# Two-layer decode kernel: row products queued behind the next unit's values, and a last projection in two rows of 256 columns

## The chip, the cores and the metric

The kernel runs on one core of a Trainium2 chip. The metric is the device time of one execution in microseconds. A core has a matrix engine (PE, with its weight loads shown apart as PEld), a vector engine (DVE), an activation engine (ACT), a general engine (POOL) and a sync engine (SP) that issues the transfers. Each engine works through its own instructions in order and waits on semaphores for the others. Matrix products land in PSUM, eight banks of 512 float32 columns on 128 partitions; everything else lies in SBUF.

## What is computed

A decode step for a batch of four tokens: attention with a cached K and V, then a gated feed-forward, and the same pair once more with the same weights and caches.

```python
def _A_ref(x, k_cache, v_cache, wq, wo):       # x (4,1,512), caches (4,8,8192,128)
    q = (x @ wq).reshape(B, Sq, 32, 128).transpose(0, 2, 1, 3)
    k = jnp.repeat(k_cache, 4, axis=1); v = jnp.repeat(v_cache, 4, axis=1)
    p = _softmax(jnp.einsum("bhqd,bhkd->bhqk", q, k) * (128 ** -0.5), axis=-1)
    o = jnp.einsum("bhqk,bhkd->bhqd", p, v)
    return o.transpose(0, 2, 1, 3).reshape(B, Sq, 32 * 128) @ wo     # wo (4096, 512)
def _B_ref(x, w_gate, w_up, w_down):           # 512 -> 1792 -> 512
    return (_silu(x @ w_gate) * (x @ w_up)) @ w_down
x = x + _A_ref(_layernorm(x), ...)
x = x + _B_ref(_layernorm(x), ...)
x = x + _A_ref(_layernorm(x), ...)
x = x + _B_ref(_layernorm(x), ...)
```

All inputs are bfloat16. The caches are 64 MB each in bfloat16 and are read in both layers, save a few pieces that stay on the chip between them.

## The kernel before

**Units.** The attention of a layer is cut into 16 units. Unit u = 4 gp + b holds two key-value heads (pair gp) of batch row b, with their 8 query heads. Its keys are one transfer of 4 MB and its values another. Layer 0 takes the units from 0 to 15, layer 1 in the order 15, 14, 13, 12, 0 to 11. The last transfers are cut into pieces: the values of the last unit come as 2048, 1536 and 512 KB. SP issues the transfers in a fixed list (`cmds`), each as soon as its slot in SBUF is free (`pump`, `freed`); the feed-forward weights of a layer follow the last values.

**A unit's steps.** DVE turns the keys in 8 pieces (`turn`, L488), PE makes the scores of each piece (`scores`, L512), DVE takes the maximum (L518, with a PE transpose L523 and L526), PE and ACT make the exponentials (`exps`, L549 to L561), DVE turns them (`turn_p`, L576), PE multiplies with the values in four parts (`products`, L643). DVE gathers the result (L687, L691), PE combines it (L696) and DVE scales it into `oT` (L701).

**The order of the work** is written out by a small planner. `blocks` holds the pieces of PE's main work, each counted at 0.9 us; the two newest are kept back (`LAG`). `line` is a queue of small steps, each with a gap; after every block the head's gap is lowered by 0.9, and it is issued when the gap is used up (`advance`). A part 3 of values puts the unit's gather and combine at the head of the line. `flush` issues steps at once, up to a tag or all of them.

**Output projection.** When the four units of a pair are done, `close_group` queues its projection with `wo`. The last pair of a layer is done directly (`project`, L767). Earlier ones are done as row products: `mix` (L721, L725) rearranges `oT`, `rows` (L747) makes eight products of 512 columns per pair, all summed in one row of bank OUTB, 4 by 512. After the last of these pairs `by_chunks` turns the row back to the layout of x: four times an ACT copy of 128 columns (L755) and a PE transpose (L757), in one step, and then DVE adds it to x (L711). Pairs 0 and 1 are queued together when pair 1 is done, with unit 7. In layer 0 pair 2 follows, and unit 13's keys, a piece of which is held in PSUM between the layers, issue all of `line` at their seventh block (`finished`, `hold`). In layer 1 pair 3 comes first, and pairs 0 and 1 are the last to go this way.

**The end.** After the last unit: `project`, the layer norm (`center`, L790 to L805, and `deviation`), gate and up products (L859), the gate function on DVE and ACT (L866 to L873), and the last projection. In layer 1 this gives x in rows straight away: `x_rows` (L785) first puts x into four quarter rows of bank STEP, each 4 by 128 on partitions 0, 32, 64 and 96, with float32 products by the identity; x_rows(0) is called between the products of the layer norm and the gate products, x_rows(1) between the up products and the last projection. Then 14 times four products (L880) add w_down; each quarter row takes 128 columns. DVE copies quarters 0 and 2 (L942), ACT 1 and 3 (L940), and SP writes the 4 by 512 result out.

Of the kernel before, what the change touches and what calls it, by code (L numbers as in the profile page):

```python
# [5 lines left out]
ACTF = mybir.ActivationFunctionType  # L6
# [97 lines left out]
def bass_interleave_layers__gqa_block_cached__swiglu_ffn__decode_kernel(  # L104
# [18 lines left out]
    P = 128  # L123
# [21 lines left out]
    with ExitStack() as es:  # L145
# [23 lines left out]
        def pick2(k):  # L169
            o = k // 2 * 2 * P + k % 2  # L170
            return slice(o, o + 2 * P - 1, 2)
# [74 lines left out]
        def bank(k):  # L246
            return ps[:, k * BANKF:(k + 1) * BANKF]
# [14 lines left out]
            assert o + b <= BANKF  # L262
            return bank(k)[rows, o + a:o + b], f"pb{k}"

        def quarter(j):
            return bank(STEP)[j * QB:j * QB + B, 0:P]

        sem = lambda name: es.enter_context(nc.semaphore(name))
        engines = {"pe": nc.tensor, "act": nc.scalar, "dve": nc.vector, "pool": nc.gpsimd, "sp": nc.sync}
# [356 lines left out]
        def values(L, u):  # L626
# [22 lines left out]
            def part(i):  # L649
                if i == 0:  # L650
                    flush(order[L][-1] if u == order[L][-2] else u)
                h = i // 2
                ts = range(i % 2 * (TB // 2), (i % 2 + 1) * (TB // 2))
                if not last or not h:
                    products(h, 0, QH, ts)
                elif i == 2:
                    gather(range(QH), ok, True)
                    fill(3)
                    products(h, 0, QH - 1, range(TB))
                    flush()  # L660
                    gather(range(QH - 1), ok2)
                else:
                    fill(1)
                    products(h, QH - 1, QH, range(TB))
                    fill(1)
                if i % 2:
                    finished(V(L, u), h * QH, (h + 1) * QH)
                if i == 3:
                    if p_name == "late":
                        freed(W_SLOT[L], NB, NB + 1)  # L670
                    done.add((L, u))
                    if last:
                        gather([QH - 1], ok3)
                        combine()
                    else:
                        line[0:0] = [[0.0, None, lambda: gather(range(QH), ok, True)], [1.3, None, combine]]
                    line.extend(behind.pop(u, []))
                    if all((L, gp * B + k) in done for k in range(B)):
                        close_group(L, gp, fill)

            into, iname = (acc2, "row") if last else (acc, "pb")

# [29 lines left out]

        def mix(gs, fill):
            C = len(gs) * H2 // NA
            at, name = place("mix", 0, NA * C * B)
            names = [OT[g] for g in gs]
            now = oT[:, gs[0] * H2:(gs[-1] + 1) * H2]
            o = now.rearrange("p (c a) b -> p a c b", a=NA)
            for j in range(NA):
                for a in range(NA):  # L720
                    T.op("pe", lambda e: e.matmul(at[a * QB:(a + 1) * QB, j * C * B:(j + 1) * C * B],  # L721
                                                  lhsT=ident[:, j::NA], rhs=o[:, a], start=True, stop=True),
                         reads=["ident"] + names, writes=[name], sig=(j == NA - 1 and a == NA - 1))
            fill(1)
            T.op("dve", lambda e: e.tensor_copy(now.rearrange("p (c j) b -> p j c b", j=NA),  # L725
                                                at.rearrange("p (j c b) -> p j c b", j=NA, c=C)),
                 reads=[name], writes=names)

        groups = [[0, 1, 2, 3], [3, 0, 1, 2]]

        def close_group(L, gp, fill):
            if gp == groups[L][-1]:
                line.extend([[0.5, None, lambda: mix([gp], fill)], [0.7, None, lambda: out_proj(gp, fill)]])
                return
            if gp == 0:
                return
            gs = [0, 1] if gp == 1 else [gp]
            line.append([0.5, None, lambda: mix(gs, fill)])
            for g in gs:
                line.append([0.9, None, lambda g=g: rows(L, g)])  # L740
            if gp == groups[L][-2]:
                line.append([1.5, None, by_chunks])

        def rows(L, gp):
            for r in range(H2):
# [3 lines left out]
                                              stop=(gp == groups[L][GP - 2] and r == H2 - 1)),  # L749
                     reads=[f"wo{gp}", OT[gp]], writes=[f"pb{OUTB}"], sig=(r == H2 - 1))  # L750

        def by_chunks():
            at, name = place("mix", 0, XB)
            for kt in range(KT):
                T.op("act", lambda e: e.activation(row, bank(OUTB)[0:B, pick2(kt)], ACTF.Copy),  # L755
                     reads=[f"pb{OUTB}"], writes=["row", "pb"])
                T.op("pe", lambda e: e.matmul(at[:, kt * B:(kt + 1) * B], lhsT=row, rhs=identf[0:B, 0:B],  # L757
                                              is_transpose=True, start=True, stop=True),
                     reads=["row", "ident"], writes=[name])
            add_to_x(at, name)  # L760

        def project(gp):
            at, name = place("out", 0, XB)
# [16 lines left out]

        def x_rows(c):
            for e_ in range(2):
                for m in range(2):
                    kt, o = 2 * c + e_, m * (P // 2)
                    T.op("pe", lambda e: e.matmul(quarter(2 * c + m)[:, e_::2], lhsT=xT[:, kt * B:(kt + 1) * B],  # L785
                                                  rhs=identf[:, o:o + P // 2], start=(e_ == 0), stop=False),
                         reads=["x", "ident"], writes=[f"pb{STEP}"], sig=(e_ == 1 and m == 1))

        def center(between=lambda: None):
            T.op("dve", lambda e: e.tensor_reduce(xs, xT[:].rearrange("p (k b) -> p b k", b=B), AX.X, ALU.add),  # L790
# [53 lines left out]
        def ffn(L):  # L844
# [29 lines left out]
            if L == 1:  # L874
                x_rows(1)
                for i, (a, b, _) in enumerate(WDS[1]):
                    for fo in range(a, b):
                        for j in range(NA):
                            o = s * SL + O_WD + fo * D + j * P
                            T.op("pe", lambda e: e.matmul(quarter(j), lhsT=hT[:, fo * B:(fo + 1) * B],  # L880
                                                          rhs=kvf[:, o:o + P], start=False, stop=(fo == FO - 1)),
                                 reads=["hT", f"wd{i}"] + rooms["wd"], writes=[f"part{j}"],
                                 sig=(fo == b - 1))
                freed(s, 4, NB)
                return
# [26 lines left out]
        for L in range(2):  # L912
            us = order[L]
            turn_of.update((u, i % 2) for i, u in enumerate(us))
            totals.clear()
            center()
            qproj(L, us[0])
            if L:
# [15 lines left out]
            ffn(L)  # L934
        assert issued[0] == len(cmds)

        for j in range(NA):
            to = xio[:, j * P:(j + 1) * P]
            if j % 2:
                T.op("act", lambda e: e.activation(to, quarter(j), ACTF.Copy), reads=[f"part{j}"], writes=[f"y{j}"])  # L940
            else:
                T.op("dve", lambda e: e.tensor_copy(to, quarter(j)), reads=[f"part{j}"], writes=[f"y{j}"])  # L942
        T.wait_res("sp", reads=[f"y{j}" for j in range(NA)])
        nc.sync.dma_start(out.rearrange("b s d -> (b s) d"), xio).then_inc(sem_out, 16)
        nc.sync.wait_ge(sem_out, 16)

# [27 lines left out]
```

## Time and profile before

| | us |
|---|---|
| median of 3 runs (lowest, highest) | 648.68 (648.66, 649.57) |
| the profiled execution | 648.87 |
| its span, first to last instruction | 647.0 |
| PE busy | 427.5 (66%) |
| DVE busy | 430.0 (66%) |
| ACT busy | 41.2 (6%) |
| key transfers in the chain that ended last | 48% |
| DVE turns of the keys (L488) in that chain | 22% |

The page names groups by line, engine, operation and shapes, with count and mean time. A matrix record's own time holds its latency; products that follow one another overlap, so a group's busy time is shorter than count times mean. Float32 products are recorded as two passes each. The granted clock is the share of full speed that PE's throttle allowed, 0.871 on the average of this execution. A line with [0.42 <-DMA ...] says that the engine sat idle for 0.42 us before it and what ended the wait. In all 272.90 MB are read, 422 GB/s over the span.

### The profile page before, as it was taken

To read this page: it belongs to the slowest core of one execution; us is meant where nothing else is said; L and a number is where in the kernel's file an instruction comes from. 1 tells how busy PE (TensorE), PEld (TensorE's weight loads), DVE (VectorE), ACT (ScalarE), POOL (GpSimd) and SP (SyncE) were. 2 spreads that over 40 slices of the span, in tenths; PEclk is the share of its full clock that TensorE was granted. 3 is DMA by queue.
4 is the path that set the end of the run, shared out by engine and by line. 5 is a ranking of instruction groups with operands and counts; after the bars stand their busy time and mean duration, and the time that the engine had idled before them with its cause. 6 is when DMAs were issued, how large, how long until landed. Compare 5 with 4: busy or idle time off the path is not lost.

```text
span 647.0 us, 7504 instructions
## 1 busy us (share of the span) xinstructions
PE 427.5 (66%) x3128; PEld 175.5 (27%) x3128; DVE 430.0 (66%) x706; ACT 41.2 (6%) x117; POOL 11.1 (2%) x43
## 2 busy tenths in 40 slices
PE   2574465555766756767857887777565577667777
PEld 2221122212222212323227332222222122222225
DVE  1585467566776666777852878878666677765964
ACT  1000000000000000001010010000000000000010
POOL 0000000000000000000000000000000000000000
PEclk9997787699878989788975899999778987879977
DMA  9999999999999999999999999999999999999996
GB/s 369 435 426 418 446 424 427 422 442 431 421 438 431 427 435 432 428 434 429 429 411 404 408 430 441 427 424 441 425 429 436 424 436 432 428 434 429 432 413 253
DMA packets 14129, 273.37 MB, mean 423 GB/s; under 512 B 1416, under 2 KB 1424, under 8 KB 5264
## 3 DMA queue, kind: packets, MB, share of 16 engines
q1 hardware_dynamic: 14096, 272.91, 99.0%
q8 instruction: 24, 0.39, 0.2%
q14 instruction: 9, 0.07, 0.0%
HBM read 272.90 MB, written 0.00 MB: 422 GB/s over the span
## 4 chain that ended last, share of the span: by engine, by line
DMA 55%; DVE 31%; PE 10%; issue 3%; ACT 0%; SPq 0%; ACTq 0%; DVEq 0%
DMA kvf<-in_A_k_cache_dram 48%; DVE kvf L488 22%; DMA kvf<-in_A_v_cache_dram 4%; PE ps L512 3%; DVE pT L576 3%; DVE pb L691 3%; PE ps L643 3%; DMA kvf<-in_B_w_down_dram 2%; PE ps L747 1%; DVE pb L687 1%; PE ps L822 1%; PE ps L859 0%; DVE tiny L518 0%; DVE scr L701 0%; DVE ps L455 0%
## 5 line engine op out<-in xcount | busy, mean ns | idle before, releaser
L512 PE MATMUL ps<-kvf,zq 128*128 128x512 bf16 x1024 | 299.9, 429 | 174.7 <-DVE kvf L488 168.3
L488 DVE STREAM_TRANSPOSE kvf<-kvf 128x1024 f32<-128x1024 f32 x246 | 289.9, 1218 | 99.0 <-DMA kvf<-in_A_k_cache_dram 98.1
L512 PEld LDWEIGHTS ps<-kvf,zq 128*128 128x128 bf16 x1024 | 91.6, 106 | 346.3 <-DVE kvf L488 249.3
L643 PE MATMUL ps<-kvf,pT 128*32 128x512 bf16 x960 | 67.5, 398 | 1.1 <-DVE pT L576 1.1
L559 ACT ACTIVATE pb<-ps,tiny 128x512 bf16<-128x512 f32 x32 | 22.0, 687 | 529.6 <-DVE tiny L557 492.9
L518 DVE TENSOR_REDUCE tiny<-ps 128x1 f32<-128x512 f32 x32 | 21.9, 685 | 34.5 <-PE ps L512 34.5
L576 DVE STREAM_TRANSPOSE pT<-pb 64x512 bf16<-64x512 bf16 x60 | 41.2, 687 | 3.1 <-ACT pb L559 2.0
L691 DVE SCALAR_TENSOR_TENSOR pb<-ps,tiny,pb 128x128 f32<-128x128 f32 x104 | 36.5, 351 | 4.5 <-PE ps L643 0.7
L643 PEld LDWEIGHTS ps<-kvf,pT 128*32 128x32 bf16 x960 | 21.3, 98 | 30.3 <-issue 14.3
L696 PEld LDWEIGHTS ps<-sel,pb 128*128 128x128 f32 x64 | 15.9, 264 | 20.0 <-DVE pb L691 13.2
L526 DVE TENSOR_REDUCE mrm<-ps 1x8 f32<-1x128 f32 x32 | 8.8, 273 | 15.1 <-PE ps L523 15.1
L502 POOL TENSOR_TENSOR zq<-scr,tiny 128x64 bf16<-128x64 bf16 x30 | 9.0, 299 | 567.2 <-PE ps L512 567.2
L696 PE MATMUL ps<-sel,pb 128*128 128x8 f32 x64 | 12.6, 270 | 7.2 <-DVE pb L691 7.2
L747 PE MATMUL ps<-wo_sb,scr 128*4 128x512 bf16 x48 | 11.3, 378 | 6.0 <-DVE scr L725 6.0
L549 PEld LDWEIGHTS ps<-mrm,tiny 128*128 128x128 f32 x60 | 12.5, 217 | 9.2 <-DVE scr L701 3.2
L549 PE MATMUL ps<-mrm,tiny 128*128 128x16 f32 x60 | 9.9, 242 | 3.4 <-ACT mrm L561 3.1
L687 DVE TENSOR_SCALAR pb<-ps,tiny 128x128 f32<-128x128 f32 x32 | 10.1, 315 | 3.0 <-PE ps L643 3.0
L711 DVE TENSOR_TENSOR xT<-xT,ps 128x16 f32<-128x16 f32 x6 | 1.0, 171 | 16.6 <-PE ps L757 11.9
L822 PE MATMUL ps<-xn,kvf 128*128 128x4 bf16 x256 | 7.6, 166 | 3.9 <-DMA kvf<-in_A_wq_dram 3.2
L523 PE MATMUL ps<-identf,tiny 128*1 128x128 f32 x32 | 8.6, 270 | 2.2 <-DVE tiny L518 2.2
L561 ACT ACTIVATE mrm<-head,tiny 128x8 f32<-128x8 f32 x32 | 9.6, 301 | 1.0
L822 PEld LDWEIGHTS ps<-xn,kvf 128*128 128x128 bf16 x256 | 7.6, 106 | 4.2 <-DMA kvf<-in_A_wq_dram 3.2
(83 smaller groups left out, 120.7 us busy)
## 6 DMA issues: line engine op xcount, KB each, us to landing
kvf<-in_A_k_cache_dram SPq DMA_DIRECT2D x28, 4096.0 KB, 30.8
kvf<-in_A_v_cache_dram SPq DMA_DIRECT2D x27, 4096.0 KB, 33.0
kvf<-in_A_v_cache_dram SPq DMA_DIRECT2D x4, 2048.0 KB, 20.0
kvf<-in_A_k_cache_dram SPq DMA_DIRECT2D x4, 2048.0 KB, 10.4
kvf<-in_A_wq_dram SPq DMA_DIRECT2D x2, 2048.0 KB, 9.8
wo_sb<-in_A_wo_dram SPq DMA_DIRECT2D x4, 1024.0 KB, 40.5
kvf<-in_B_w_gate_dram SPq DMA_DIRECT2D x2, 1792.0 KB, 24.4
kvf<-in_A_v_cache_dram SPq DMA_DIRECT2D x2, 1536.0 KB, 32.0
```

Of the source, the lines that this page charges most:

```text
L488: T.op("dve", lambda e: e.transpose(w, w), reads=[f"s{s}.{q}"], writes=[f"s{s}.{q}"])
L512: T.op("pe", lambda e: e.matmul(bank(bk)[:, 0:SW], lhsT=zq[:, z0:z0 + P], rhs=w[:, :, c // 2, :, c % 2], start=(q == 0 and c == 0), stop=( ...
L518: T.op("dve", lambda e: e.tensor_reduce(mx[:], bank(bk)[:, 0:SW], AX.X, ALU.max), reads=[f"pb{bk}"], writes=["mx"])
L549: T.op("pe", lambda e: e.matmul(at, lhsT=ones, rhs=mrm[:, i * H2:(i + 2) * H2], start=True, stop=True), reads=[f"m8{i}", "rsm", "onesf"], ...
L559: T.op("act", lambda e: e.activation(pb[:], bank(bk)[:, 0:SW], ACTF.Exp, bias=nm, accum_out=rs), reads=[f"pb{bk}", "nm"], writes=PB + ["rs"])
L576: T.op("dve", lambda e: e.transpose(dst, pb[hp]), reads=["pb", "row"], writes=[name])
L643: T.op("pe", lambda e: e.matmul(bank(k)[j * QB:(j + 1) * QB, q0 * Dh:q1 * Dh], lhsT=p_t[:, t, h, :], rhs=v[:, q0:q1, t, :], start=((last o ...
L687: T.op("dve", lambda e: e.tensor_scalar(into, o, own[:, q:q + 1], None, op0=ALU.mult), reads=[f"pb{k}", "own"], writes=["row"] if last els ...
L691: T.op("dve", lambda e: e.scalar_tensor_tensor(into, o, own[:, q:q + 1], into, op0=ALU.mult, op1=ALU.add), reads=[f"pb{k}", "own", iname], ...
L696: T.op("pe", lambda e: e.matmul(at, lhsT=into, rhs=sel[:], start=True, stop=True), reads=[iname, "sel"], writes=[name])
L747: T.op("pe", lambda e: e.matmul(bank(OUTB)[0:B, 0:D], lhsT=oT[:, h, :], rhs=wo_sb[:, h, :], start=(gp == groups[L][0] and r == 0), stop=(g ...
L822: T.op("pe", lambda e: e.matmul(at[:, h * B:(h + 1) * B], lhsT=wq_sb[:, kt, h * Dh:(h + 1) * Dh], rhs=xn[:, kt * B:(kt + 1) * B], start=(k ...
```

## The change

Two things are changed.

First, the row products and the turning back. `close_group` still queues `mix`. The row products of a closed pair no longer go into `line` as steps of 0.9 but into a list `later`, which part 3 of the next unit's values takes up: it issues them at once, behind that unit's products. The turning back is no longer one step but five (`upright`), each with a gap of 0.9: a step transposes the copy of the step before and makes the next copy; the last one adds to x. In layer 1 these five are appended to the line after the next unit's own steps. For pair 2 of layer 0 the row products are one step of 0.7 in the line, followed by the five. The transposes land in the last 16 columns of bank LNB.

Second, the last projection. The four quarter rows become two half rows of 256 columns, on partitions 0 and 64. `x_rows` makes two products of 128 columns per call in place of four of 64, L880 two products of 256 columns for each of the 14 slices in place of four of 128, and the result is copied by one DVE and one ACT copy of 256 columns in place of two of 128 on each.

```diff
-        def quarter(j):
-            return bank(STEP)[j * QB:j * QB + B, 0:P]
+        def half_row(c):
+            return bank(STEP)[2 * c * QB:2 * c * QB + B, 0:2 * P]
...
                 if i == 3:
+                    more = later.pop(0)() if later else []
...
                         close_group(L, gp, fill)
+                    line.extend(more)
...
         def mix(gs, fill):
...
+            mixed.update(gs)
...
+        mixed, later = set(), []
...
             gs = [0, 1] if gp == 1 else [gp]
             line.append([0.5, None, lambda: mix(gs, fill)])
-            for g in gs:
-                line.append([0.9, None, lambda g=g: rows(L, g)])
-            if gp == groups[L][-2]:
-                line.append([1.5, None, by_chunks])
+            turned_back = upright() if gp == groups[L][-2] else []
+
+            def in_rows():
+                while gp not in mixed:
+                    line.pop(0)[2]()
+                for g in gs:
+                    rows(L, g)
+                return turned_back
+            if turned_back and not L:
+                line.extend([[0.7, None, in_rows]] + turned_back)
+            else:
+                later.append(in_rows)
...
-        def by_chunks():
-            at, name = place("mix", 0, XB)
-            for kt in range(KT):
-                T.op("act", lambda e: e.activation(row, bank(OUTB)[0:B, pick2(kt)], ACTF.Copy),
-                     reads=[f"pb{OUTB}"], writes=["row", "pb"])
-                T.op("pe", lambda e: e.matmul(at[:, kt * B:(kt + 1) * B], lhsT=row, rhs=identf[0:B, 0:B],
-                                              is_transpose=True, start=True, stop=True),
-                     reads=["row", "ident"], writes=[name])
-            add_to_x(at, name)
+        def upright():
+            at, name = bank(LNB)[:, 4 * P - XB:4 * P], f"pb{LNB}"
+
+            def step(kt):
+                if kt:
+                    T.op("pe", lambda e: e.matmul(at[:, (kt - 1) * B:kt * B], lhsT=row, rhs=identf[0:B, 0:B],
+                                                  is_transpose=True, start=True, stop=True),
+                         reads=["row", "ident"], writes=[name])
+                if kt < KT:
+                    T.op("act", lambda e: e.activation(row, bank(OUTB)[0:B, pick2(kt)], ACTF.Copy),
+                         reads=[f"pb{OUTB}"], writes=["row", "pb"])
+                else:
+                    add_to_x(at, name)
+            return [[0.9, None, lambda kt=kt: step(kt)] for kt in range(KT + 1)]
...
         def x_rows(c):
             for e_ in range(2):
-                for m in range(2):
-                    kt, o = 2 * c + e_, m * (P // 2)
-                    T.op("pe", lambda e: e.matmul(quarter(2 * c + m)[:, e_::2], lhsT=xT[:, kt * B:(kt + 1) * B],
-                                                  rhs=identf[:, o:o + P // 2], start=(e_ == 0), stop=False),
-                         reads=["x", "ident"], writes=[f"pb{STEP}"], sig=(e_ == 1 and m == 1))
+                kt = 2 * c + e_
+                T.op("pe", lambda e: e.matmul(half_row(c)[:, e_::2], lhsT=xT[:, kt * B:(kt + 1) * B], rhs=identf[:],
+                                              start=(e_ == 0), stop=False),
+                     reads=["x", "ident"], writes=[f"pb{STEP}"], sig=(e_ == 1))
...
-                        for j in range(NA):
-                            o = s * SL + O_WD + fo * D + j * P
-                            T.op("pe", lambda e: e.matmul(quarter(j), lhsT=hT[:, fo * B:(fo + 1) * B],
-                                                          rhs=kvf[:, o:o + P], start=False, stop=(fo == FO - 1)),
-                                 reads=["hT", f"wd{i}"] + rooms["wd"], writes=[f"part{j}"],
+                        for c in range(2):
+                            o = s * SL + O_WD + fo * D + 2 * c * P
+                            T.op("pe", lambda e: e.matmul(half_row(c), lhsT=hT[:, fo * B:(fo + 1) * B],
+                                                          rhs=kvf[:, o:o + 2 * P], start=False, stop=(fo == FO - 1)),
+                                 reads=["hT", f"wd{i}"] + rooms["wd"], writes=[f"part{c}"],
                                  sig=(fo == b - 1))
...
-        for j in range(NA):
-            to = xio[:, j * P:(j + 1) * P]
-            if j % 2:
-                T.op("act", lambda e: e.activation(to, quarter(j), ACTF.Copy), reads=[f"part{j}"], writes=[f"y{j}"])
+        for c in range(2):
+            to = xio[:, 2 * c * P:2 * (c + 1) * P]
+            if c:
+                T.op("act", lambda e: e.activation(to, half_row(c), ACTF.Copy), reads=[f"part{c}"], writes=[f"y{c}"])
             else:
-                T.op("dve", lambda e: e.tensor_copy(to, quarter(j)), reads=[f"part{j}"], writes=[f"y{j}"])
+                T.op("dve", lambda e: e.tensor_copy(to, half_row(c)), reads=[f"part{c}"], writes=[f"y{c}"])
```

## The prediction

> **What bounds the kernel now.** I read the page first, for what is busy and what the chain of waits is made of.
>
> ```profile
> q1 hardware_dynamic: 14096, 272.91, 99.0%
> ...
> DMA 55%; DVE 31%; PE 10%; issue 3%; ACT 0%; SPq 0%; ACTq 0%; DVEq 0%
> ```
>
> The DMA queue fills 16 engines for 99.0% of the span, and DMA is the largest part of the chain. So work in the middle of the span is worth time only if it delays a transfer or the tail. To see where the compute stands against the transfers I read the timeline, first where the turning back of layer 1 lies.
>
> ```profile
> 574.24 2.37 DVE L488 STREAM_TRANSPOSE kvf<-kvf 128x1024 f32<-128x1024 f32 x2 [4.42 <-DMA kvf<-in_A_k_cache_dram]
> ...
> 586.84 1.89 PE L747 MATMUL ps<-wo_sb,scr 128*4 128x512 bf16 x8 [1.48 <-DVE scr L725]
> ...
> 591.56 0.27 ACT L755 ACTIVATE pb<-ps 4x128 f32<-4x128 f32 x1 [8.89 <-PE ps L747]
> ...
> 594.30 0.17 DVE L711 TENSOR_TENSOR xT<-xT,ps 128x16 f32<-128x16 f32 x1 [7.52 <-PE ps L757]
> 594.39 0.68 DVE L518 TENSOR_REDUCE tiny<-ps 128x1 f32<-128x512 f32 x1
> 594.99 2.36 DVE L488 STREAM_TRANSPOSE kvf<-kvf 128x1024 f32<-128x1024 f32 x2
> ```
>
> At 574.24 DVE had waited 4.42 us for unit 9's keys: there the transfers lead. Then come sixteen row products (the first eight in the line at 586.84), and the four ACT copies and PE transposes of the turning back, which hold PE and DVE until 594.30: DVE runs them in order, so unit 9's maximum (594.39) and unit 10's first turn (594.99) stand behind them. Unit 10's keys are two transfers of 4096 KB after unit 9's (values of 8 between them). 8.39 MB at 425 GB/s is 19.7 us, so they land near 574.2 + 19.7 = 594.0 (an estimate; 594.2 with its semaphore). The stall of some 4 us therefore delays the compute by 594.99 - 594.2 = 0.8 us only. Then the end of the same timeline.
>
> ```profile
> 632.34 2.81 DVE L691 SCALAR_TENSOR_TENSOR pb<-ps,tiny,pb 128x128 f32<-128x128 f32 x7
> 632.44 0.45 PEld L643 LDWEIGHTS ps<-kvf 128*32 128x32 bf16 x16 [0.42 <-DMA kvf<-in_A_v_cache_dram]
> ...
> 633.68 0.23 PEld L643 LDWEIGHTS ps<-kvf 128*32 128x32 bf16 x16 [0.38 <-DMA kvf<-in_A_v_cache_dram]
> ...
> 638.54 0.60 PE L785 MATMUL ps<-identf,xT 128*4 128x64 f32 x8
> ...
> 639.07 0.91 PE L859 MATMUL ps<-xn,kvf 128*128 128x4 bf16 x28
> ...
> 640.26 2.38 PE L859 MATMUL ps<-xn,kvf 128*128 128x4 bf16 x84
> ...
> 642.57 0.59 PE L785 MATMUL ps<-identf,xT 128*4 128x64 f32 x8
> 642.80 0.21 DVE L873 TENSOR_TENSOR pb<-pb,ps 128x56 bf16<-128x56 f32 x1
> ...
> 643.07 1.66 PE L880 MATMUL ps<-kvf,pb 128*4 128x128 bf16 x56
> 644.76 0.59 DVE L942 CAST pb<-ps 4x128 bf16<-4x128 f32 x2 [1.75 <-PE ps L880]
> 644.79 0.56 ACT L940 ACTIVATE pb<-ps 4x128 bf16<-4x128 f32 x2 [3.11 <-PE ps L880]
> ```
>
> At 632.44 and 633.68 PE waits for the last two pieces of the last unit's values: the transfers lead again, and whatever was gained before is cut off here. The last value piece has landed by 633.68, and all that follows, 13.3 us to the end of the span, is a chain of compute. The windows show the state of that chain.
>
> ```profile
> 632.00:634.00 2.00, 1.91 (x36) 0.68 (x34) 1.75 (x7) 0.00 (x0) 0.00 (x0) 1.00 0.99 407
> ...
> 640.00:642.00 2.00, 2.00 (x68) 2.00 (x69) 0.69 (x4) 0.81 (x3) 0.00 (x0) 0.50 0.56 211
> 642.00:644.00 2.00, 2.00 (x72) 1.79 (x73) 0.87 (x3) 0.00 (x0) 0.00 (x0) 0.50 0.11 42
> 644.00:646.00 2.00, 0.73 (x28) 0.44 (x20) 0.56 (x2) 0.54 (x2) 0.00 (x0) 0.50 0.00 0
> ```
>
> In the columns (busy us and instructions of PE, PEld, DVE, ACT, POOL, then granted clock, DMA share, GB/s) the transfers run at full share at 632 and die out by 644, and the clock granted to PE, 1.00 at 632, is 0.50 from 640 to the end. The tail is compute at half clock, and this is where the change has its second half.
>
> **The change part by part.**
>
> *Row products of units 0 to 7, behind the next values.* The instructions are the same: 16 matmuls of 512 columns (L747). In layer 1 they move from before unit 8's values to behind them, near 590 to 593.5. Cover: PE then waits for unit 10's keys, due at 594.2. Without it they would cost 16 x 0.216 = 3.5 us (0.216 from L747: eight in 1.89 us, one of them 0.378, so (1.89 - 0.378) / 7). In layer 0 they move from 212.8 behind unit 8's values near 235, where PE next sits idle 5.04 us before unit 10's turned keys (240.24); layer 1's first group, eight products, moves from 433.0 to about 438, behind a 0.86 us gap, and may delay PE by 1 us. On SP the key and value transfers are issued from semaphores that PE raises; they shift by up to 3.5 us, earlier or later. A key transfer takes a median 30.8 us from issue to landing, mostly queueing behind others, so none arrives later: 0. POOL's placing of q and its memset wait for PE and DVE in the same places: 0.
>
> *Turning back, spread.* In layer 1 the four copies and transposes and the addition to x become five steps, one per block of unit 10's and 11's scores. Each PE step is 0.22 us, each copy 0.27, between blocks where DVE's turns (1.22 us each) set the pace; a transpose finds its copy made a block earlier. Behind a late step would stand, on ACT, the next exponential, and on DVE, unit 11's turns: neither is near. In layer 0 the half-kept keys empty the whole line at unit 13's seventh block, so all steps run there back to back as now: 0. What is gained is the 0.8 us at 594.99 and unit 9's maximum and its transpose reduction, taken while DVE waits: about 1 us earlier through unit 11's turns. What is late next: the values. The last unit's first piece lands (1536 + 512 KB, 2.10 MB at 425, 4.9 us before 633.6) near 628.7, against 629.19 where it is first used now; and the second at 632.4. DVE's gathering runs without a break from 631.97; its fifth step started at 633.57, while its products, behind the 632.44 wait, were done by 633.27. Started at once after them (0.08 us for the semaphore) it is 0.22 us earlier, no more. I take -0.20, bounds -0.22 and 0.
>
> *x in rows (L785), before the projection.* It is called twice with four float32 matmuls (eight records), two of 64 columns on each of two column groups; now two of 128 columns on one group. The last projection gives the column price: 56 matmuls in 1.66 us, 0.308 for one, four at a time, so 13 rounds in 1.66 - 0.31 = 1.35 us, 0.104 a round of 128 columns; half of L747's 2.37 columns a ns gives 0.108. I take 0.107. L785's eight records take 0.60 with 0.31 for one, so three rounds in 0.29, 0.10 each: a 64-column float32 pass costs as much as 128 bf16 columns. Four passes are 0.43 now and 0.85 then. The first call stands straight before the gate products at 639.07: +0.43, bounds 0 and +0.43. The second (642.57) ends its passes near 643.0, and L880 could start at 643.07 anyhow, after DVE's last multiplication (642.80 + 0.21): 0.08 covered, +0.35, bounds the same. Both calls move everything behind them.
>
> *Last projection (L880).* From 56 matmuls of 128 columns, four column groups side by side, to 28 of 256, two side by side. Each group streams 14 x 256 in place of 14 x 128 columns: 14 x 0.213 = 2.99 against 14 x 0.107 = 1.49 us, +1.50. All of it is on the path: nothing else is left. Bounds: if the price were per instruction, 28 x 0.027 = 0.75, that is -0.75; if the halves did not overlap at all, 28 x 0.213 = 5.97, +4.5. I take +1.50, because rounds of four in step are what the trace has. The last weights (256 KB) were needed about 644.3 and are needed later: no new wait.
>
> *Copies.* Two of 4x128 on DVE take 0.59 and two on ACT 0.56 (a second one 0.28 and 0.27); now one of 4x256 on each. No such shape is in the trace; a DVE cast of 256 columns out of PSUM (L842) takes 0.414, ACT's 512 columns 0.687 against 0.269 for 128, so about 0.41 for 256. Bounds -0.30 (a second copy for nothing) and 0; I take -0.15 by these nearest rows. The single output DMA waits for two names, not four: 0.
>
> **Sum:** +0.43 + 0.35 + 1.50 - 0.15 - 0.20 = +1.93 us. The profiled execution took 648.87 us, so 650.80. The median of the three runs lies 0.19 below it: 650.6, +0.30%.
>
> **The rivals.**
>
> *The clock comes back during the projection.* A denser tail (x in rows 0.85 us and 2.99 us of columns from 643.0 on) could be granted full clock partway. At half of the remaining columns saved from 645 on, 0.9 us: 649.7. From the second call on it would be 0.43 + 1.49 in place of 0.85 + 2.99, nearly the present time: 648.7. For it: clocks return elsewhere, 0.50 at 628 to 630 and 1.00 at 632. Against it: the windows from 640 to 646 all show 0.50, and the dense part is short. The Trainium skill, "TensorE: Matmul & The Clock Gate", section "What's actually happening", has a free-running window of about 3.4 us which, once busy, releases the clock; by that rule the outcome hangs on where a window starts, and the 0.50 in the rows of now does not contradict it.
>
> *Price per instruction.* This is the rival on the other side. L859 spends (2.38 - 0.17) / 83 = 0.027 us a matmul of 4 columns, and L880 0.104 / 4 = 0.026 with 128: as if only the number counted. Then the projection is -0.75, each x in rows (four records fewer at 0.05) -0.2, the copies -0.15, upstream -0.20: 648.7 - 1.5 = 647.2. Against it: sixteen value products of 512 columns (L643, 594.20) take 1.05 us with 0.40 for one, 0.217 a round of four, twice the price per instruction at full clock, and L747's alone 0.216. It decides if a matmul of 256 columns costs under about 0.05 us, not 0.107. The same page of the Trainium skill, section "Wait — 56ns, not 53.3ns?", puts a floor near 25 ns under small matmuls; by that floor alone the 28 would take an estimated 0.7 us, as this rival says.
>
> *A colder end.* If PE, ahead and waiting for the last values, has not its clock back at 632, the 384-column products take 1.3 in place of 0.83 us and the small ones after them a little longer: +0.5, 651.1.
>
> **How the numbers follow.** Forecast (half clock throughout, 650.1 to 651.1): 0.72. Clock back partway, 649.7: 0.10; from early on, 648.7: 0.04. Per instruction, 647.2: 0.05. Colder end, 651.1 and above: 0.06. Halves that overlap less than hoped, 651.5 and above: 0.03. About 0.2% (1.3 us: 647.4 to 650.0) is what a measurement of this kernel tells from no change; its own three runs span 0.91. Slower is 0.72 + 0.06 + 0.03 = 0.81; same 0.10 + 0.04 = 0.14; faster 0.05. The range from 649.3 to 651.4 leaves out the per-instruction case, the early clock and the worst overlap, and reaches over the other two.
>
> **What would show it.** The value wait at 632.44 stays there but is longer, and L711 and L518 no longer stand at 594.30 in a stall; unit 10's first turn comes at 594.2, released by its DMA. From the last wait at 633.68 to the end of the span 15.2 in place of 13.3 us: the gate products begin 0.4 later, L880 takes 3.2 in place of 1.66 us, the copies 0.4 in place of 0.59. Wrong I am if L880's rounds of two stay at 0.107, if the clock row shows 1.00 there, or if a transfer lands later than now.

## The result, and the profile after

| | before, us | changed, us |
|---|---|---|
| median (lowest to highest) of 8 runs each | 648.85 (648.38 to 649.57) | 650.60 (649.29 to 651.76) |
| the profiled execution | 648.87 | 650.83 |
| its span | 647.0 | 649.0 |

The changed kernel is slower by 0.26%: the ratio is 1.0026, with an interval of 95% from 1.0016 to 1.0035. The forecast was 650.6. Its parts did not all come out as its sum has them, though, and the profile shows which.

The page of the changed kernel, the queue and the chain of waits. DMA's part of the chain went from 55% to 61%, DVE's from 31% to 24%. These are shares of one execution's chain: with the moved row products alone, an experiment further down, they are 57% and 29%, so they do not measure the change. Where the compute waits now is read from the timeline.

```profile
q1 hardware_dynamic: 14096, 272.91, 98.7%
...
DMA 61%; DVE 24%; PE 11%; issue 3%; SPq 0%; ACT 0%; DVEq 0%
```

Its timeline where the row products of layer 1 now lie, behind unit 8's values:

```profile
590.41 3.62 PE L759 MATMUL ps<-wo_sb,scr 128*4 128x512 bf16 x16
594.27 2.37 DVE L488 STREAM_TRANSPOSE kvf<-kvf 128x1024 f32<-128x1024 f32 x2 [4.35 <-DMA kvf<-in_A_k_cache_dram]
```

All sixteen row products (L759, L747 before) are done by 594.03, and unit 10's first key turn starts at 594.27, released by its transfer after a wait of 4.35 us; before, it started at 594.99 behind the turning back. Further on in the same timeline, and below it unit 9's value products in the kernel before:

```profile
612.73 0.17 DVE L713 TENSOR_TENSOR xT<-xT,ps 128x16 f32<-128x16 f32 x1 [1.51 <-PE ps L769]
...
619.24 1.05 PE L643 MATMUL ps<-kvf,pT 128*32 128x512 bf16 x16
...
634.83 0.23 PEld L643 LDWEIGHTS ps<-kvf 128*32 128x32 bf16 x16 [0.41 <-DMA kvf<-in_A_v_cache_dram]
```

```profile
618.43 1.05 PE L643 MATMUL ps<-kvf,pT 128*32 128x512 bf16 x16
```

The last step of the spread turning back, the addition to x (L713), kept DVE waiting 1.51 us for PE. Unit 9's value products (L643) start at 619.24; before, they started at 618.43. The 0.7 us gained at unit 10's keys are gone again, and 0.8 more with them. It cost nothing in the end: the last value piece came at 634.83, in the kernel before at 633.68. Then the tail:

```profile
639.20 0.60 PE L801 MATMUL ps<-identf,xT 128*4 128x128 f32 x4
...
639.73 0.90 PE L875 MATMUL ps<-xn,kvf 128*128 128x4 bf16 x28
...
643.23 0.80 PE L801 MATMUL ps<-identf,xT 128*4 128x128 f32 x3
...
643.89 3.11 PE L896 MATMUL ps<-kvf,pb 128*4 128x256 bf16 x27
646.93 0.41 DVE L959 CAST pb<-ps 4x256 bf16<-4x256 f32 x1 [3.26 <-PE ps L896]
647.03 0.38 ACT L957 ACTIVATE pb<-ps 4x256 bf16<-4x256 f32 x1 [4.69 <-PE ps L896]
```

The first x in rows (L801) takes 0.53 us to the gate products (L875), exactly as before (638.54 to 639.07), though its products have 128 columns in place of 64. The last projection (L896, the row has 27 of its 28 products) takes 3.11 us in place of 1.66 and the copies 0.41 and 0.38 in place of 0.59 and 0.56. The windows of this execution (after the length of the window: PE, PEld, DVE, ACT, POOL busy and instructions, the granted clock, DMA share, GB/s) show why some of it differs from the forecast:

```profile
608.00:610.00 2.00, 1.15 (x4) 0.39 (x4) 2.00 (x2) 0.26 (x1) 0.70 (x2) 0.77 0.99 426
610.00:612.00 2.00, 2.00 (x7) 0.60 (x5) 1.22 (x2) 0.27 (x1) 0.00 (x0) 0.50 1.03 442
612.00:614.00 2.00, 2.00 (x10) 0.78 (x9) 1.27 (x3) 0.00 (x0) 0.00 (x0) 0.88 0.91 393
...
644.00:646.00 2.00, 2.00 (x23) 1.85 (x20) 0.00 (x0) 0.00 (x0) 0.00 (x0) 0.50 0.01 5
646.00:648.00 2.00, 1.00 (x11) 0.59 (x6) 0.41 (x1) 0.38 (x1) 0.00 (x0) 0.84 0.00 0
```

A window of 2 us with a mean clock c between 0.50 and 1.00 holds (1 - c) x 2 x 2 us of half clock. So the clock fell to half for some 3.4 us around 610 ((1 - 0.77) x 2 x 2 + 2 + (1 - 0.88) x 2 x 2), which is where DVE waited for PE's step. In the tail it came back during 646 to 648, at the end of the last projection. The first x in rows, at 639.2, still had it full.

Where the 2.0 us of span come from, by the starts of the same instructions in both profiles:

| from | to | before | changed | difference |
|---|---|---|---|---|
| first instruction | last value piece taken up | 633.68 | 634.83 | +1.15 |
| last value piece | combine (L696, L698) | 1.53 | 1.25 | -0.28 |
| combine | sum for the layer norm | 2.81 | 2.80 | -0.01 |
| sum for the layer norm | first gate product | 1.05 | 0.85 | -0.20 |
| gate product | second x in rows | 3.50 | 3.50 | 0.00 |
| second x in rows | later copy of the result (ACT) | 2.22 | 3.80 | +1.58 |
| later copy | output transfer issued | 0.64 | 0.45 | -0.19 |
| output transfer | end of span | 1.57 | 1.52 | -0.05 |

The -0.20 ahead of the first gate product is the layer norm's sum, whose two products (L793 before, L809 now) took 0.59 us at half clock and 0.39 at full. The +1.15 in the first row was not foreseen, and the prediction had named a transfer that lands later as a sign of being wrong. Either the moved row products delay the transfers, or it is a difference between executions. The experiments had to settle that, and which half of the change costs what.

### The profile page after: what moved, and what is told of

It is laid out like the page before. It is cut to its first block, busy times and chain, and to the rows that moved or that the text cites. A ratio compares the mean times of both kernels' runs of the same rounds, so it can differ in the third digit from the quotient of the medians.

```text
span 649.0 us, 7429 instructions
## 1 busy us (share of the span) xinstructions
PE 428.9 (66%) x3092; PEld 176.1 (27%) x3092; DVE 430.2 (66%) x705; ACT 41.0 (6%) x116; POOL 11.1 (2%) x43
## 4 chain that ended last, share of the span: by engine, by line
DMA 61%; DVE 24%; PE 11%; issue 3%; SPq 0%; ACT 0%; DVEq 0%
DMA kvf<-in_A_k_cache_dram 49%; DVE kvf L488 18%; DMA kvf<-in_A_v_cache_dram 11%; PE ps L512 5%; DVE pT L576 3%; PE ps L643 2%; DMA kvf<-in_B_w_down_dram 2%; DVE pb L693 2%; PE ps L838 1%; DVE pb L689 0%; PE ps L875 0%; PE ps L896 0%; DVE scr L703 0%; PE ps L523 0%; PE ps L759 0%
## 5 line engine op out<-in xcount | busy, mean ns | idle before, releaser
L643 PE MATMUL ps<-kvf,pT 128*32 128x512 bf16 x960 | 66.4, 399 | 1.6 <-DVE pT L576 1.6
L643 PEld LDWEIGHTS ps<-kvf,pT 128*32 128x32 bf16 x960 | 21.0, 98 | 31.9 <-issue 16.6
L698 PEld LDWEIGHTS ps<-sel,pb 128*128 128x128 f32 x64 | 15.7, 263 | 22.3 <-DVE pb L693 15.8
L698 PE MATMUL ps<-sel,pb 128*128 128x8 f32 x64 | 13.0, 277 | 9.3 <-DVE pb L693 9.3
L759 PE MATMUL ps<-wo_sb,scr 128*4 128x512 bf16 x48 | 11.0, 379 | 1.5 <-DVE scr L728 1.5
L713 DVE TENSOR_TENSOR xT<-xT,ps 128x16 f32<-128x16 f32 x6 | 1.0, 171 | 10.6 <-PE ps L769 5.9
```

Source lines behind the costliest of these rows:

```text
L643: T.op("pe", lambda e: e.matmul(bank(k)[j * QB:(j + 1) * QB, q0 * Dh:q1 * Dh], lhsT=p_t[:, t, h, :], rhs=v[:, q0:q1, t, :], start=((last o ...
L698: T.op("pe", lambda e: e.matmul(at, lhsT=into, rhs=sel[:], start=True, stop=True), reads=[iname, "sel"], writes=[name])
L759: T.op("pe", lambda e: e.matmul(bank(OUTB)[0:B, 0:D], lhsT=oT[:, h, :], rhs=wo_sb[:, h, :], start=(gp == groups[L][0] and r == 0), stop=(g ...
```

## The experiments

Their times are compared with runs of the kernel before on the same chip, whose median was 648.63 in both comparisons.

**One half of the change alone.** The second half: `half_row`, `x_rows`, the last projection and the copies as in the changed kernel, everything else as before.

```diff
-        def quarter(j):
+        def half_row(c):
... (x_rows, last projection, copies as in the change; close_group, rows, by_chunks as before)
```

> The kernel before with the second half of the change alone: half rows of 256 columns in x in rows and in the last projection, one copy on each engine; row products and turning back as before. Theory (each column group streams its own columns, so two groups take twice as long as four): the last projection 3.1 us in place of 1.66, the second call of x in rows some 0.3 to 0.4 longer, the first 0 to 0.4 longer as the clock stands, copies 0.12 less; the time 1.5 to 2.1 us above before, about 650.6. Rival (the moved row products cost, because they shift the transfers: in the changed kernel's profile the last value piece landed at 634.8 in place of 633.7): this kernel only 0.8 to 1.0 us above before, the last value piece at 633.7.

Measured: 650.32 (649.47 to 650.75), ratio 1.0024 (1.0014 to 1.0033).

```profile
633.70 0.23 PEld L643 LDWEIGHTS ps<-kvf 128*32 128x32 bf16 x16 [0.32 <-DMA kvf<-in_A_v_cache_dram]
...
642.40 0.80 PE L784 MATMUL ps<-identf,xT 128*4 128x128 f32 x3
...
642.89 0.37 PE L879 MATMUL ps<-kvf,pb 128*4 128x256 bf16 x1
...
643.06 3.34 PE L879 MATMUL ps<-kvf,pb 128*4 128x256 bf16 x27
646.23 0.41 DVE L941 CAST pb<-ps 4x256 bf16<-4x256 f32 x1 [3.39 <-PE ps L879]
646.43 0.38 ACT L939 ACTIVATE pb<-ps 4x256 bf16<-4x256 f32 x1 [4.92 <-PE ps L879]
```

The last value piece is taken up at 633.70, as before, and from the second x in rows (642.40) to the later copy it takes 4.03 us in place of 2.22. The median's slowing by 1.7 us is here in full. In this one profile the tail from the last value piece grew by 1.4 us (13.32 to 14.70); the first x in rows and the layer norm's sum still ran at full clock in it, as in the changed kernel's profile. The rival's 649.4 to 649.6 lies at the lower end of the interval (649.5 to 650.8 in time); what speaks against it is the first half alone:

**The first half alone:** the row products and the turning back of the changed kernel, four quarter rows and four copies as before.

```diff
-        def half_row(c):
+        def quarter(j):
... (x_rows, last projection, copies as before; later, in_rows, upright as in the change)
```

> The changed kernel with its second half undone: row products and turning back moved and spread, the last projection in four quarter rows with four copies. Theory (the gain upstream is cut off by the last values): between 0.3 us below before and no difference, 648.5 to 648.9; unit 10's first key turn released by its transfer at about 594.2, from the last value wait to the combine some 0.2 to 0.3 us shorter. Rival (the moved rows shift the transfers): 1 us above before, with the last value piece again near 634.8.

Measured: 648.63 (647.69 to 649.50), ratio 1.0002 (0.9993 to 1.0010).

```profile
593.26 2.37 DVE L488 STREAM_TRANSPOSE kvf<-kvf 128x1024 f32<-128x1024 f32 x2 [4.40 <-DMA kvf<-in_A_k_cache_dram]
...
610.18 0.17 DVE L713 TENSOR_TENSOR xT<-xT,ps 128x16 f32<-128x16 f32 x1
...
616.70 1.05 PE L643 MATMUL ps<-kvf,pT 128*32 128x512 bf16 x16
...
633.25 0.23 PEld L643 LDWEIGHTS ps<-kvf 128*32 128x32 bf16 x16 [0.41 <-DMA kvf<-in_A_v_cache_dram]
...
642.78 1.66 PE L897 MATMUL ps<-kvf,pb 128*4 128x128 bf16 x56
```

No difference in time, and the last value piece is there at 633.25, earlier than in the kernel before; from it to the combine it is 1.26 us in place of 1.53, as expected. In all six other profiles with the same moved row products the last value piece was taken up between 633.20 and 633.88. So the moved row products do not delay the transfers, and the 1.15 us of the changed kernel's profile belong to that execution. Here the addition to x (L713) found its transpose ready, since the clock was full from 579.1 to 623.5, and unit 9's value products started at 616.70, where the kernel before had 618.43.

One place where executions drift apart is a window at the start of layer 1, of the kernel before, of the changed one and of the second half alone:

```profile
360.00:380.00 20.00, 17.64 (x101) 6.96 (x100) 15.34 (x20) 1.08 (x3) 0.60 (x2) 0.97 1.01 428
```

```profile
360.00:380.00 20.00, 18.70 (x101) 7.21 (x100) 15.34 (x20) 1.08 (x3) 0.60 (x2) 0.92 1.00 412
```

```profile
360.00:380.00 20.00, 18.66 (x101) 7.20 (x100) 15.33 (x20) 1.08 (x3) 0.60 (x2) 0.92 1.00 410
```

The transfers moved 428, 412 and 410 GB/s there at granted clocks of 0.97, 0.92 and 0.92 (the last three columns are clock, share and GB/s). 16 GB/s over 20 us are 0.32 MB, 0.75 us of transfer. Row products had been moved in only one of the two slow ones. But this window does not explain the 1.15 us: the second half alone lost as much in it and had its last value piece at 633.70, as the kernel before. Nor does the loss always go with the clock: twice the products, the next experiment, moved 427 GB/s there at a clock of 0.93. That PE's later key scores free the slots later is a reading that was not tried by itself.

**Twice the products on the same two rows:**

```diff
-                        for c in range(2):
-                            o = s * SL + O_WD + fo * D + 2 * c * P
-                            ... matmul(half_row(c), ..., rhs=kvf[:, o:o + 2 * P], ...)
+                        for m in range(2):
+                            for c in range(2):
+                                o = s * SL + O_WD + fo * D + (2 * c + m) * P
+                                ... matmul(half_row(c)[:, m * P:(m + 1) * P], ..., rhs=kvf[:, o:o + P], ...)
```

> The changed kernel with each 256-column product of the last projection as two of 128 columns on the same half row: 56 products in place of 28, two column groups as before. Theory (price by columns per group): the last projection still about 3.1 us, the time as the changed kernel's, 650.6 within 0.5. Rival (something in a product of 256 columns is dear beyond its columns, or only the number of products counts): 56 products take 1.5 us as in the kernel before, the time 649.0 to 649.2.

Measured: 650.39 (649.80 to 651.00), ratio 1.0027 (1.0017 to 1.0037).

```profile
642.43 0.80 PE L801 MATMUL ps<-identf,xT 128*4 128x128 f32 x3
...
643.10 3.20 PE L897 MATMUL ps<-kvf,pb 128*4 128x128 bf16 x54
...
646.34 0.38 ACT L958 ACTIVATE pb<-ps 4x256 bf16<-4x256 f32 x1 [4.79 <-PE ps L897]
```

56 products of 128 columns on two column groups take as long as 28 of 256: from the second x in rows (642.43) to the later copy 3.91 us, against 2.22 for the same 56 products on four groups. The number of products is not the price.

**One row of 512 columns:**

```diff
         def half_row(c):
-            return bank(STEP)[2 * c * QB:2 * c * QB + B, 0:2 * P]
+            return bank(STEP)[0:B, 2 * c * P:2 * (c + 1) * P]
... (last projection: one product of 512 columns for each slice; both copies on DVE)
```

> The changed kernel with one row of 512 columns on one column group: 14 products of 512 columns, x in rows on the same group in two calls as in the changed kernel, both copies of 256 columns on DVE one after the other. Theory (columns per group): 14 x 0.427 = 6.0 us for the last projection at half clock, 3.0 more than the changed kernel, and the second copy 0.4 more: about 654.0; 1 to 2 us less if the longer run of wide products brings the clock back. Rival (groups do not matter once the products are wide): 0.4 us above the changed kernel, 651.0.

Measured: 652.30 (651.75 to 653.59), ratio 1.0054 (1.0038 to 1.0069).

```profile
644.15 5.28 PE L895 MATMUL ps<-kvf,pb 128*4 128x512 bf16 x14
...
649.46 0.74 DVE L958 CAST pb<-ps 4x256 bf16<-4x256 f32 x2 [5.68 <-PE ps L895]
```

One group takes 5.28 us, where two take 3.11 (for 27 of 28 products) and four 1.66. At half clock all the way it would have been 6.0; the profile has the clock back for the last 1.1 us. It is 1.7 us below the 654.0 of half clock, within the 1 to 2 allowed for that, and 1.3 above the rival's 651.0. The second copy cost 0.33 (0.74 against 0.41).

**A busier PE ahead of the last projection:**

```diff
                     if bk == gb and fo == FO // 2:
                         deviation(zero_sb, "zero")
+                    if L and bk == ub:
+                        stream(1)
```

> The changed kernel with fourteen more products of 512 columns, whose result is not used, one ahead of each slice of the up products of layer 1, to make PE busy before the last projection. It is for the duration of the last projection, not for the time, which it lengthens by 3 to 6 us. Theory (columns at the granted clock): the clock is back at 1.00 before the last projection, whose 28 products then take 1.5 to 1.7 us, and the second call of x in rows 0.43 in place of 0.85. Rival (the 28 products are held by something other than PE's column rate, such as their weight loads): 3 us at full clock too.

Measured, one run: 653.52.

```profile
637.83 1.02 PE L801 MATMUL ps<-identf,xT 128*4 128x128 f32 x4
...
638.78 0.91 PE L877 MATMUL ps<-xn,kvf 128*128 128x4 bf16 x28
...
647.56 0.60 PE L801 MATMUL ps<-identf,xT 128*4 128x128 f32 x4
...
647.94 1.75 PE L898 MATMUL ps<-kvf,pb 128*4 128x256 bf16 x28
...
649.73 0.38 ACT L959 ACTIVATE pb<-ps 4x256 bf16<-4x256 f32 x1 [8.33 <-PE ps L898]
```

```profile
636.00:638.00 2.00, 1.97 (x36) 1.37 (x34) 0.41 (x3) 0.00 (x0) 0.00 (x0) 0.55 1.02 386
...
646.00:648.00 2.00, 1.76 (x30) 1.24 (x31) 0.21 (x1) 0.00 (x0) 0.00 (x0) 0.89 0.00 0
```

```profile
647.50:649.50 2.00, 2.00 (x37) 1.76 (x34) 0.21 (x1) 0.00 (x0) 0.00 (x0) 1.00 0.00 0
```

At full clock the same 28 products take 1.75 us, and from the second x in rows to the later copy it is 2.17 us, not 3.80. The expectation had 1.5 to 1.7 us for the products. At half clock throughout, with the second half alone, they took 3.51 us (642.89 to 646.40), twice 1.75: the price goes by columns per group at the granted clock. The first x in rows, here at half clock, takes 0.95 us to the gate products (637.83 to 638.78): the +0.42 that the changed kernel's own profile did not show. The fourteen products that bring the clock back cost more than they save: this run is 2.9 us above the changed kernel's median. The rule of a window of some 3.4 us (the Trainium skill, "TensorE: Matmul & The Clock Gate", section "What's actually happening") fits: the half-clock stretch of this execution lasted from 636.2 to 646.4, three times 3.41, and ended with the first such window that the fourteen products, from 641.3 on, had filled. The same stretch lasted 6.8 us, twice 3.41, in the changed kernel (639.8 to 646.6), with the second half alone (639.7 to 646.5) and with twice the products (639.2 to 646.0), and it ended with the first 3.41 us that the wide products filled. A PE that is busy with small products did not bring the clock back: in the kernel before, PE is busy for 2.00 of 2.00 us at 640 and at 642, for the most part with products of 4 columns, and the clock stays at 0.50. What PE must do for the clock to come back was not tried apart.

**Two copies on each engine:**

```diff
-        for c in range(2):
-            to = xio[:, 2 * c * P:2 * (c + 1) * P]
+        for j in range(NA):
+            to, c, m = xio[:, j * P:(j + 1) * P], j // 2, j % 2
... (half row 0 in two copies on DVE, half row 1 in two on ACT)
```

> The changed kernel with each half row copied in two copies of 128 columns, both halves of a row on one engine. Theory: 0.15 us more between the last product and the output transfer (two copies of 0.28 in place of one of 0.41), too little to see in the time, so read from the profile: DVE 0.59 and ACT 0.56 again. Rival (a second copy is nearly free, or a wide one is as dear as two): no difference of over 0.03 us there.

Measured, one run: 649.93.

```profile
645.88 0.48 DVE L960 CAST pb<-ps 4x128 bf16<-4x128 f32 x2 [3.38 <-PE ps L896]
646.08 0.43 ACT L958 ACTIVATE pb<-ps 4x128 bf16<-4x128 f32 x2 [4.92 <-PE ps L896]
```

Both expectations missed. Two copies of 128 columns right behind one another take 0.07 us more on DVE and 0.05 more on ACT than the single copy of 256, not 0.15 to 0.2. In the kernel before, two copies took 0.59 and 0.56. So of the 0.18 us that the single copies save on each engine, two copies back to back already save 0.11 (0.59 to 0.48) and 0.13 (0.56 to 0.43). In the kernel before, the second copy had a wait of its own and read other partitions than the first; here it has no wait of its own and reads the same partitions. Which of the two costs the time was not tried apart.

**The stall of the turning back, doubled where it was:**

```diff
-                line.append([1.5, None, by_chunks])
+                line.append([1.5, None, lambda: by_chunks(2 if L else 1)])
...
-            for kt in range(KT):
+            for kt in list(range(KT)) * times:
```

> The kernel before with the turning back of layer 1 done twice over in its one step: four more copies and transposes, the second four making the same values again; nothing else is changed. Theory (the compute of the kernel before reaches the last values with almost nothing to spare, so that every further us of this stall is an us of the time): four more pairs of 0.58 us, 2.3 us above before, 650.9, and no wait for the last values left. Rival (the transfers hide such a stall): no difference, 648.6.

Measured: 650.84 (650.03 to 651.21), ratio 1.0033 (1.0021 to 1.0044), 2.2 us.

```profile
596.41 0.17 DVE L711 TENSOR_TENSOR xT<-xT,ps 128x16 f32<-128x16 f32 x1 [9.82 <-PE ps L757]
596.50 0.68 DVE L518 TENSOR_REDUCE tiny<-ps 128x1 f32<-128x512 f32 x1
...
597.10 2.36 DVE L488 STREAM_TRANSPOSE kvf<-kvf 128x1024 f32<-128x1024 f32 x2
```

```profile
633.95 0.45 PEld L643 LDWEIGHTS ps<-kvf 128*32 128x32 bf16 x16 [0.42 <-issue]
...
635.04 0.23 PEld L643 LDWEIGHTS ps<-kvf 128*32 128x32 bf16 x16 [0.23 <-issue]
```

Unit 10's first turn starts 2.1 us later than before, and at 633.95 and 635.04 nothing waits for the last values any more. A further us of this stall was worth an us: the kernel before stood with its compute just at the edge of its transfers.

**The spread turning back, doubled:** the first half alone again, with nine steps in place of five.

```diff
-            turned_back = upright() if gp == groups[L][-2] else []
+            turned_back = upright(2 if L else 1) if gp == groups[L][-2] else []
... (upright: the four copies and transposes twice, one step each)
```

> Row products and turning back moved and spread, the last projection in four quarter rows as before, and the spread turning back of layer 1 done twice over, in nine steps in place of five. Theory (spread over unit 10's and 11's blocks it costs nothing, and the transfers end the wait): no difference to the kernel before, 648.3 to 648.9. Rival (the stall is only moved, each pair costs its 0.5 us wherever it stands): 2.3 us above before, 650.9.

Measured: 648.38 (647.75 to 649.77), ratio 0.9998 (0.9989 to 1.0008).

```profile
615.97 0.17 DVE L713 TENSOR_TENSOR xT<-xT,ps 128x16 f32<-128x16 f32 x1
...
633.58 0.23 PEld L643 LDWEIGHTS ps<-kvf 128*32 128x32 bf16 x16 [0.41 <-DMA kvf<-in_A_v_cache_dram]
```

The same additional work that cost 2.2 us in one step costs nothing in spread ones, and PE waits for the last value piece as before. None of these kernels is clear of the kernel before on the fast side.

## Why the prediction was right, and where its sum was not

**Row products: 0.** Right. With them moved alone the ratio is 1.0002, and no transfer was late for them.

**Turning back spread: -0.20, about 1 us earlier upstream.** In part. The first turn of unit 10 came with its transfer, as said (594.27, released by the keys). From the last value piece to the combine it was 1.25 us in place of 1.53, -0.28 where -0.20 was put, with -0.22 as the bound. The time does not show it: 1.0002, with an interval that holds the -0.03% of 0.20 us, and 0. What failed is the sentence that a late step stands near nothing. In three profiles, the changed kernel's, that of twice the products and that of the one row, the clock was at half around 608 to 612, and DVE waited 1.51, 1.32 and 1.75 us for the last transpose with unit 11's turns behind it. The rows of the last two:

```profile
612.62 0.17 DVE L713 TENSOR_TENSOR xT<-xT,ps 128x16 f32<-128x16 f32 x1 [1.32 <-PE ps L769]
```

```profile
612.20 0.17 DVE L713 TENSOR_TENSOR xT<-xT,ps 128x16 f32<-128x16 f32 x1 [1.75 <-PE ps L769]
```

In the profiles of the first half alone, of the four copies, of the busier PE and of the spread twice, with full clock there, it did not wait. Unit 9's value products started at 616.70 to 616.87 in the first three of these, over 1.5 us before the 618.43 of the kernel before, and at 618.77 to 619.24 where the clock fell. So the early compute was eaten up where the clock fell there; in the changed kernel's profile the last values came later still.

**First x in rows: +0.43.** The size is right at half clock (0.95 against 0.53 us), but in the changed kernel's profile the clock was still full at 639.2, and the term was 0, as it was in the profiles of the second half alone, of twice the products and of the four copies. The forecast had taken over the clock's place from the profile before, where it fell at 637.6.

**Second x in rows and last projection: +0.35 and +1.50, 1.85 together.** Measured to the later copy: +1.81 with the second half alone (4.03 against 2.22), +1.69 with twice the products, +1.58 in the changed kernel. The mechanism, a price by columns per column group at the granted clock, is shown by one, two and four groups, by twice the products and by full clock; the two halves do stream side by side. Where the clock stayed at half until the end the size was right: with the second half alone it came back at 646.5, after the last product. In the changed kernel it came back at 646.6, 0.4 us before the later copy, and gave back 0.2 to 0.3 us: the rival of the clock's return in a weak form, in place of its 0.9.

**Copies: -0.15.** -0.18 on each engine, -0.19 from the later copy's start to the issue of the output transfer. The reason given, a price by columns, was only a part of it: more of it was saved by two copies right behind one another.

**The sum: +1.93 against +1.96 in the profiles and +1.75 in the medians.** In the profile this is partly luck: the tail from the last value piece grew by 0.85 us (13.32 to 14.17, where the forecast had 15.2), and the transfers of that execution were late by 1.15. Over runs, the second half alone has +1.7 us, the first half 0, and these two make up the +1.75. The term that was too large in the changed kernel's profile is the first x in rows, taken at half clock. That the forecast of 650.6 is the measured median to the tenth is luck too: it was added to a median of 648.68 of three runs, and eight runs of the kernel before have 648.85.

**The other rivals.** A price per instruction is refuted by twice the products, and halves that do not overlap (5.97 us in the prediction) by the 3.51 us of the 28 products at half clock throughout. A colder end did not show: the clock was full from 630 to 638 in the changed kernel.

**Left open:** whether the 0.28 us to the combine are worth anything in time (too small for these runs), and what makes the transfers of one execution up to 1.6 us later than those of another (633.20 to 634.83 for the last value piece in kernels with the same moved row products); the window at the start of layer 1 does not account for it.

## What to carry to other kernels

Small outputs that sit on separate column groups of PE stream side by side: joining four into two wider rows halved the number of instructions and doubled the time here, and it is the columns per group, at the granted clock, that are to be counted. A stall of compute that ran just at the edge of its transfers was worth nothing here when removed and its full price when doubled, so a kernel's profile should be asked for the waits on both sides of it. Work spread over later blocks was cheap only while the engine that waits for it found it done; look for what stands behind its last step.

## What was not expected of the hardware

The granted clock's place is not a property of the kernel: the half-clock stretches lie elsewhere in each execution (around 610 in the changed kernel's profile and in none of the first half's), and a term priced at one clock is right in one execution and nothing in the next. Eight runs of the changed kernel spread over 2.5 us, the kernel before over 1.2. Two copies out of PSUM right behind one another took 0.48 us on DVE and 0.43 on ACT, 0.05 to 0.07 us over one copy of double width; two copies from different partitions, each with a wait of its own, took 0.59 and 0.56.
